# Other PSUM banks for the last 20 steps, products moved behind P V, x loaded in chunks, splits parted anew, and Q/K rows stored so that a head is one transfer

## The chip, the cores and the metric

The kernel runs on one core of a Trainium2 chip. A core has a matrix engine (TensorE, "PE" in the profile), a vector engine (VectorE, "DVE"), an engine for activations (ScalarE, "ACT"), a general one (GpSimd, "POOL") and one that mostly issues transfers (SyncE, "SP"). They run side by side and wait for each other by semaphores. Matrix products are written to PSUM, which has eight banks; 128 rows of 512 float32 numbers fill one. The metric is device time in microseconds (us), the median of several runs; lower is better.

## The reference, cut to what matters

One input `x` of 2048 tokens and 512 features goes through two branches, mixed by a gate for each token:

```
g = sigmoid((x * gate_w).sum(-1, keepdims=True))
# branch a: attention, 32 heads of 16 features, softmax over all 2048 keys
q, k, v = split(x @ wqkv)
p = softmax(q @ k.T / 4)            # for each head, 2048 x 2048
a = (p @ v) @ wo
# branch b: the two tokens of highest score r = x @ w_r get an FFN, the others pass
y = (silu(x_sel @ w_gate) * (x_sel @ w_up)) @ w_down * sigmoid(r_sel)
b = x, with y added at the two tokens
out = g * a + (1 - g) * b
```

Nearly all of the work is the scores, their exponentials and P V: 32 heads with 2048 x 2048 scores each.

## The kernel before, in words

**Number format.** Products that need more than the matrix engine's fast float32 form are made of parts: an operand is split into a high part and the rest (`split`: ScalarE makes the high part, VectorE or GpSimd subtracts), and high x high, low x high and high x low are added up in PSUM. So a projection or an output product is 3 matmuls per 128 rows of the inner dimension.

**Start.** `load_x` fetches x transposed in four blocks of 512 tokens, each in four pieces of 128 x 512 from a matrix with rows of 2048 tokens; SP issues all of them, between the two halves of the first weights. `split_x` splits each piece, three on VectorE and the fourth on GpSimd. Fourteen matmuls on zeros (L228) run while the first data arrive. `proj` makes K and Q of the first 8 heads for a block of tokens (12 matmuls, an eviction with a split of the result, `ev`). The V weights are split once the first three projections are recorded (L254). Then 21 lead steps hold the row maxima of the first unit (`m_lead`) and the V products (`v_part`).

**Main part.** Heads go in pairs and queries in halves: 32 units, each of 16 steps over 128 keys, 512 steps in all. A step `s` makes S^T for 128 keys and 1024 queries of the two heads: four matmuls (`s_piece`, L669), with two heads in the two row halves of the array, and one exponential (ScalarE, L670) for each, into `P[s]`. P V (`av_mm`) follows two steps later. The row maxima that the softmax subtracts are found ahead, from products of their own (`m_piece`, L589) that VectorE reduces (L593). `ORDER` writes out the order of S^T pieces (s), maxima (m), P V (A) and fillers (f). A filler is a part of other work: the projections of later heads, the small FFN, the output products with `wo`.

**PSUM.** The tiles are: `st`, three banks; `mxa`, one tile of two banks; `mxb`, `fl` and `av`, one bank each. In the main part S^T uses `st`, the maxima use `mxa` and `mxb`, fillers use `fl` and P V uses `av`.

**The last 20 steps.** When the maxima are done (steps 492 to 511), a loop of its own makes the four S^T pieces of a step, P V of two steps earlier, and in every second step a filler between the second and the third piece; there they are output products of the last heads (`wo_last`), which VectorE adds to the result (`finish`). The fourth piece of each step goes into `mxb`, the others into `st`: four banks.

**End.** `tail` makes the last normalisation and the products of the last heads' output. Blocks 10 and 11 go through the two halves of `mxa`, block 9 through `st`; then four blocks, each of three products (high part, low part, high part), a finish and a store.

**Transfers.** Q and K go through a scratch in DRAM, a plane of high parts and a plane of low parts. A matmul needs each head's rows three times 16: for K high, low, high, for Q high, high, low. `load_k` and `load_q` make that of two transfers for each head, one of 32 rows and one of 16. Each queue issues its transfers in program order, and the order of work between engines comes from a layer that records which instruction reads and writes which tile and sets the waits.

## Time and profile before

| | us |
|---|---|
| median of three runs | 1420.77 (1420.66 to 1420.93) |
| the profiled execution | 1419.9 |
| its span, which the trace covers | 1417.9 |
| first to last matmul of the start, before the maxima (0 to 27.2) | 27.2 |
| lead steps (27.2 to 91) | 63.8 |
| main part (91 to 1359) | 1268.0 |
| last 20 steps' S^T (1359 to 1402.1) | 43.1 |
| end (1402.1 to 1417.9) | 15.8 |

In the span TensorE has 1410.2 us of busy time (99%), VectorE 1288.8 (91%), ScalarE 1170.9 (83%) and GpSimd 320.4 (23%). How to read the rows: in rows in order of time the first number is the start in us, the second the length, then the engine, the line, the operation, output and inputs by the program's names, and the count where rows were merged. What stands in brackets is the idle time of the engine before it and what ended it. Starts and ends of matmuls overlap, as they are pipelined.

### The profile page before, as it was taken

What the parts mean: (1) busy time and instruction counts of PE and PEld (TensorE: products, weight loads), DVE (VectorE), ACT (ScalarE), POOL (GpSimd) and SP (SyncE); (2) the same over time, 40 slices, a digit from 0 to 9 for tenths busy, and PEclk for the clock granted to TensorE, in tenths of its full rate; (3) what the DMA queues carried; (4) which work ended last, traced back from release to release, by engine and by line L of the source; (5) the groups of instructions that cost most, each with busy time, mean ns of one, the idle gap of its engine ahead of it and who ended that gap; (6) DMA issues with size and microseconds to landing.
All of it is one profiled execution on the core that took longest, in us unless ns stands there. A gap on an engine that the chain in (4) does not pass through costs nothing.

```text
span 1417.9 us, 24172 instructions
## 1 busy us (share of the span) xinstructions
PE 1410.2 (99%) x9113; PEld 630.7 (44%) x9113; DVE 1288.8 (91%) x1532; ACT 1170.9 (83%) x2276; POOL 320.4 (23%) x337
## 2 busy tenths in 40 slices
PE   9999999999999999999999999999999999999998
PEld 6654444444444444444444444434444444444433
DVE  6889999999999999999999999999999999999943
ACT  5568888888888888888888888888888888888986
POOL 4851101102000001200000100043722322234411
PEclk9999999999999999999999999999999999999999
DMA  8601121212223221312222332424322131012012
GB/s 242 235 27 51 30 42 31 66 34 51 46 64 97 62 54 31 68 30 65 58 83 54 87 82 78 105 58 120 83 46 54 34 69 28 26 31 58 10 35 93
DMA packets 51592, 92.87 MB, mean 65 GB/s; under 512 B 14208, under 2 KB 21376, under 8 KB 49844
## 3 DMA queue, kind: packets, MB, share of 16 engines
q1 hardware_dynamic: 51188, 91.02, 24.4%
q8 instruction: 72, 1.18, 0.4%
q0 software_dynamic: 288, 0.30, 0.1%
q14 instruction: 44, 0.36, 0.1%
HBM read 63.77 MB, written 28.57 MB: 65 GB/s over the span
## 4 chain that ended last, share of the span: by engine, by line
PE 98%; DVE 0%; DMA 0%; ACT 0%; SPq 0%; issue 0%; POOL 0%; DVEq 0%; ACTq 0%
PE av L679 36%; PE st L669 24%; PE mxa L589 12%; PE mxb L589 10%; PE fl L154 6%; PE fl L508 4%; PE st L298 3%; PE st L154 2%; PE mxa L624 1%; PE fl L399 1%; DMA xs<-xT 0%; PE fl L437 0%; DVE acc L559 0%; DVE Mr L593 0%; PE mxa L508 0%; PE mxb L624 0%
## 5 line engine op out<-in xcount | busy, mean ns | idle before, releaser
L670 ACT ACTIVATE P<-st 128x512 f32<-128x512 f32 x2028 | 1065.6, 599 | 191.4 <-PE st L669 108.0
L593 DVE TENSOR_REDUCE Mr<-mxa 128x2 f32<-128x1024 f32 x655 | 795.7, 1215 | 2.6 <-PE mxa L589 2.5
L679 PE MATMUL av<-P,V 128*32 128x512 f32 x4096 | 545.6, 605 | 0.0
L669 PE MATMUL st<-Qx,Kx 50*128 50x512 f32 x2028 | 536.5, 444 | 0.8 <-ACT P L670 0.6
L593 DVE TENSOR_REDUCE Mr<-mxb 128x1 f32<-128x512 f32 x654 | 450.9, 689 | 61.0 <-PE st L669 17.1
L669 PEld LDWEIGHTS st<-Qx,Kx 50*128 50x128 f32 x2028 | 279.0, 184 | 239.6 <-ACT P L670 223.8
L589 PE MATMUL mxb<-Kx,Qx 48*128 48x512 f32 x654 | 325.1, 497 | 0.0
L589 PE MATMUL mxa<-Kx,Qx 48*128 48x512 f32 x1310 | 294.7, 417 | 0.0
L589 PEld LDWEIGHTS mxb<-Kx,Qx 48*128 48x128 f32 x654 | 119.5, 183 | 273.7 <-DVE Mr L593 273.7
L589 PEld LDWEIGHTS mxa<-Kx,Qx 48*128 48x128 f32 x1310 | 124.8, 183 | 43.6 <-DVE Mr L593 2.6
L679 PEld LDWEIGHTS av<-P,V 128*32 128x32 f32 x4096 | 81.2, 108 | 139.3 <-issue 133.2
L205 POOL TENSOR_SCALAR ev<-pe 128x512 fp32r<-128x512 f32 x24 | 35.7, 1490 | 411.6 <-ACT pe L203 411.6
L475 POOL TENSOR_TENSOR acc<-acc,w 128x512 f32<-128x512 f32 x36 | 46.1, 1280 | 202.1 <-ACT w L474 202.0
L77 POOL TENSOR_SCALAR hl<-m 128x16 fp32r<-128x16 f32 x31 | 7.8, 252 | 294.1 <-DVE m L640 294.1
L154 PE MATMUL fl<-xh,wh 128*128 128x512 f32 x96 | 42.9, 447 | 0.0
L154 PE MATMUL fl<-xh,wl 128*128 128x512 f32 x96 | 40.4, 421 | 0.0
L508 PE MATMUL fl<-woh,ahl 128*128 128x512 f32 x96 | 35.2, 447 | 0.0
L559 DVE SCALAR_TENSOR_TENSOR acc<-fl,gg,acc 128x512 f32<-128x512 f32 x11 | 8.2, 747 | 27.9 <-PE fl L508 27.9
L629 DVE TENSOR_REDUCE Mr<-mxa 128x2 f32<-128x1024 f32 x21 | 25.7, 1222 | 8.4 <-PE mxa L624 8.4
L154 PE MATMUL fl<-xl,wh 128*128 128x512 f32 x96 | 32.6, 421 | 0.0
L300 ACT ACTIVATE V<-st 128x512 f32<-128x512 f32 x16 | 9.6, 600 | 27.8 <-PE st L298 27.8
L206 POOL TENSOR_TENSOR ev<-pe,ev 128x512 fp32r<-128x512 f32 x24 | 30.8, 1284 | 2.0
(192 smaller groups left out, 780.0 us busy)
## 6 DMA issues: line engine op xcount, KB each, us to landing
q_scr<-ev SPq DMA_DIRECT2D x15, 512.0 KB
Kx<-k_scr SPq DMA_DIRECT2D x30, 256.0 KB
Qx<-q_scr SPq DMA_DIRECT2D x54, 128.0 KB
k_scr<-ev SPq DMA_DIRECT2D x13, 512.0 KB
Qx<-q_scr SPq DMA_DIRECT2D x70, 64.0 KB
xs<-xT SPq DMA_DIRECT2D x16, 256.0 KB
xn<-x SPq DMA_DIRECT2D x4, 1024.0 KB
Qx<-hr SPq DMA_DIRECT2D x256, 2.0 KB
```

The source lines that it names most:

```text
L154: nc.tensor.matmul(ps, a[:, i, c, :], b[nb][:, c, :], start=n == 0, stop=n == 11)
L205: nc.gpsimd.tensor_scalar(ev[:, 0], t, 1.0, None, op0=OP.mult)
L206: nc.gpsimd.tensor_sub(ev[:, 1], t, ev[:, 0].bitcast(F32))
L298: nc.tensor.matmul(ps, a[nb][:, c, sl], b[:, c, :], start=c == 0 and n == 0, stop=c == 3 and n == 2)
L475: nc.gpsimd.tensor_add(a, a, w)
L508: nc.tensor.matmul(ps, a[:, sl], b[:a.shape[0], c, :], start=first and n == 0, stop=last and n == 2)
L589: nc.tensor.matmul(dst, Qx[u % 3][64 * j:64 * j + 48, t * 128:t * 128 + 128], k_of(u, t // 4)[64 * j:64 * j + 48, c * 512:c * 512 + 512], ...
L593: nc.vector.tensor_reduce(Mr[:, g0:g0 + (2 if r == 1 else 1)], MX[r - 1], axis=AX.X, op=OP.max, negate=True)
L629: nc.vector.tensor_reduce(*r, axis=AX.X, op=OP.max, negate=True)
L669: nc.tensor.matmul(ps, k, q, start=True, stop=True)
L670: nc.scalar.activation(P[s][:, 2 * j + c, :], ps, AF.Exp)
L679: nc.tensor.matmul(AV[0][32 * ct:32 * ct + 32, :], V[:, kt, h * VW:h * VW + 32], P[s][:, ct, :], start=kt == 0, stop=kt == KT - 1)
```

## The change

- **Banks of the last 20 steps.** S^T now goes through six banks in turn, two for each half of a step: two of `st`, then one of `st` and `mxb`, then the two halves of a `mxa` tile.
- **Products.** In these steps the filler comes after P V instead of between the second and the third S^T piece.
- **x.** The host lays x out in contiguous chunks of 128 x 512. Two of the first four chunks are issued by ScalarE.
- **Splits.** All four pieces of x are split by ScalarE and VectorE. The V weights are split in two halves, after the projections of K block 2 and K block 3, with the low part on GpSimd.
- **Scratch.** It holds three rows for each feature in the order in which they are needed, so that each head's 48 rows are one transfer (but for the first pair's Q, whose scratch is read as before in two). A store is two transfers instead of one, and writes a third row.
- **Smaller ones.** Ten matmuls on zeros instead of fourteen; `split_at` of the first output group three steps later; in `tail` block 11 finished by VectorE alone, the high products of two blocks ahead of the low ones, and the last block finished and stored in two halves over two queues.

```diff
-    qk_scr = {n: dram.tile([2, D, S], F32R, name=f"{n}_scr") for n in "qk"}
+    qk_scr = {n: dram.tile([D, 3, S], F32R, name=f"{n}_scr") for n in "qk"}
...
         for c in range(4):
-            nc.sync.dma_start(xst[nb][:, c], ap(xT, c * 128 * S + nb * 512, [[S, 128], [1, 512]]))
+            eng = nc.scalar if nb == 0 and c % 2 == 0 else nc.sync
+            eng.dma_start(xst[nb][:, c], ap(xT, (nb * 4 + c) * 128 * 512, [[512, 128], [1, 512]]))
...
-            split(xh[nb][:, c], xl[nb][:, c], xst[nb][:, c], lo_engine=nc.gpsimd if c == 3 else None)
+            split(xh[nb][:, c], xl[nb][:, c], xst[nb][:, c])
...
     def store_ev(g, which, nb, ev):
-        nc.sync.dma_start(
-            ap(qk_scr[which], g * 128 * S + nb * 512, [[S, 128], [D * S, 2], [1, 512]]).bitcast(F32), ev.bitcast(F32))
+        e = ev.bitcast(F32)
+        for i, src in ((0, e), (2, e[:, 0, :])) if which == "k" else ((0, e[:, 0:1, :].to_broadcast([128, 2, 512])), (2, e[:, 1, :])):
+            d = ap(qk_scr[which], (g * 384 + i) * S + nb * 512, [[3 * S, 128], [S, 2 - i // 2], [1, 512]])
+            nc.sync.dma_start(d.bitcast(F32), src)
...
-    for _ in range(14):
+    for _ in range(10):
         nc.tensor.matmul(wps, warm[:, :128], warm, start=True, stop=True)
...
-    for c in range(4):
-        split(wv[1][:, c], wv[2][:, c], wvs[:, c], lo_engine=nc.gpsimd if c % 2 else None)
...
-            nc.sync.dma_start(t[64 * j:64 * j + 32, :], ap(qk_scr["k"], o, [[S, 16], [D * S, 2], [1, S]]).bitcast(F32))
-            nc.sync.dma_start(t[64 * j + 32:64 * j + 48, :], ap(qk_scr["k"], o, [[S, 16], [1, S]]).bitcast(F32))
+            nc.sync.dma_start(t[64 * j:64 * j + 48, :], ap(qk_scr["k"], o, [[S, 48], [1, S]]).bitcast(F32))
...
     def s_piece(s, j, c):
...
-        ps = mxb_tile() if s > STEPS - LEAD and c == 1 and j == 0 else st_tile()
+        n = (2 * s + c) % 3
+        if s <= STEPS - LEAD or n == 0 or (n == 1 and j):
+            ps = st_tile()
+        elif n == 1:
+            ps = mxb_tile()
+        else:
+            if j:
+                MX[2] = mxa_tile()
+            ps = MX[2][:, 1 - j]
         nc.tensor.matmul(ps, k, q, start=True, stop=True)
         nc.scalar.activation(P[s][:, 2 * j + c, :], ps, AF.Exp)
...
         late_wo(1)
-        acc_add(11, pw[1], gg)
+        finish(11, pw[1])
...
-        for t in range(4):
-            for n, (a, b) in enumerate(((0, 0), (1, 0), (0, 1))):
-                nc.tensor.matmul(banks[t], hl[a][:, t * 128:t * 128 + 128], wz[0][:, b, :], start=n == 0, stop=n == 2)
-            finish(12 + t, banks[t])
-            store(12 + t)
+        for t, n in ((0, 0), (0, 1), (1, 0), (1, 1), (0, 2), (1, 2), (2, 0), (2, 1), (2, 2), (3, 0), (3, 1), (3, 2)):
+            a, b = ((0, 0), (0, 1), (1, 0))[n]
+            nc.tensor.matmul(banks[t], hl[a][:, t * 128:t * 128 + 128], wz[0][:, b, :], start=n == 0, stop=n == 2)
+            if n == 2 and t < 3:
+                finish(12 + t, banks[t])
+                store(12 + t)
+        a = acc[3][:, 3, :]
+        for i, eng in enumerate((nc.scalar, nc.sync)):
+            c = slice(256 * i, 256 * i + 256)
+            nc.vector.scalar_tensor_tensor(a[:, c], banks[3][:, c], gg[:, 15:16], a[:, c], op0=OP.mult, op1=OP.add)
+            eng.dma_start(out[15 * 128:, c], a[:, c])
...
-        at_step(now[0] + 10, split_at, 0, (0, 1))
+        at_step(now[0] + 13, split_at, 0, (0, 1))
...
     for w, nb in (("k", 2), ("k", 3), ("q", 1), ("q", 2)):
         proj0(w, nb)
+        if w == "k":
+            for c in (2 * nb - 4, 2 * nb - 3):
+                split(wv[1][:, c], wv[2][:, c], wvs[:, c], lo_engine=nc.gpsimd)
...
             start_step(s)
             for i in range(4):
-                if i == 2 and (s - count["s"] // 4) % 2 == 0:
-                    next(fills, None)
                 s_piece(s, 1 - i % 2, i // 2)
         p_v(s - 2)
+        if (s - count["s"] // 4) % 2 == 0 and s < STEPS:
+            next(fills, None)
         end_step(s)
...
-        "xT": np.ascontiguousarray(x.T), "x": x, "wqkv": wqkv,
+        "xT": np.ascontiguousarray(x.T.reshape(4, 128, 4, 512).transpose(2, 0, 1, 3)), "x": x, "wqkv": wqkv,
```

More of the change, by code (lines that the diff above doesn't have):

```diff
@@ L260, in load_k @@
         for j in range(2):
-            o = (g * 128 + r + 16 * j) * S
+            o = (g * 128 + r + 16 * j) * 3 * S
             t = Kx[pair % 2 if pair < PAIRS - 1 else 2].bitcast(F32)
-            nc.sync.dma_start(t[64 * j:64 * j + 32, :], ap(qk_scr["k"], o, [[S, 16], [D * S, 2], [1, S]]).bitcast(F32))
-            nc.sync.dma_start(t[64 * j + 32:64 * j + 48, :], ap(qk_scr["k"], o, [[S, 16], [1, S]]).bitcast(F32))
+            nc.sync.dma_start(t[64 * j:64 * j + 48, :], ap(qk_scr["k"], o, [[S, 48], [1, S]]).bitcast(F32))
     def load_q(u):
@@ L271, in load_q @@
             for j in range(2):
-                o = (pair * 32 + 16 * j) * S + q0
+                o = (pair * 32 + 16 * j) * 3 * S + q0
                 t = Qx[u % 3][:, i * n:i * n + n].bitcast(F32)
-                nc.sync.dma_start(t[64 * j:64 * j + 32], ap(qk_scr["q"], o, [[S, 16], [0, 2], [1, n]]).bitcast(F32))
-                nc.sync.dma_start(t[64 * j + 32:64 * j + 48], ap(qk_scr["q"], D * S + o, [[S, 16], [1, n]]).bitcast(F32))
+                if pair:
+                    nc.sync.dma_start(t[64 * j:64 * j + 48], ap(qk_scr["q"], o, [[S, 48], [1, n]]).bitcast(F32))
+                else:
+                    nc.sync.dma_start(t[64 * j:64 * j + 32], ap(qk_scr["q"], o, [[3 * S, 16], [S, 2], [1, n]]).bitcast(F32))
+                    nc.sync.dma_start(t[64 * j + 32:64 * j + 48], ap(qk_scr["q"], o + 2 * S, [[3 * S, 16], [1, n]]).bitcast(F32))
     def k_of(u, c):
@@ L667, in s_piece @@
         q = Qx[u % 3][64 * j:64 * j + 50, c * 512:c * 512 + 512]
-        ps = mxb_tile() if s > STEPS - LEAD and c == 1 and j == 0 else st_tile()
+        n = (2 * s + c) % 3
[3 more added lines that the diff above has]
+            ps = mxb_tile()
+        else:
+            if j:
+                MX[2] = mxa_tile()
+            ps = MX[2][:, 1 - j]
         nc.tensor.matmul(ps, k, q, start=True, stop=True)
```

## The prediction

> **What bounds the kernel now.** I read the page first, then the busy time by stage, then the instructions in order of time at both ends, where the edits lie.

> ```profile
> span 1417.9 us, 24172 instructions
> PE 1410.2 (99%) x9113; PEld 630.7 (44%) x9113; DVE 1288.8 (91%) x1532; ACT 1170.9 (83%) x2276; POOL 320.4 (23%) x337
> ```

> ```profile
> 8.75:27.20 18.45, 18.45 (x78) 14.32 (x78) 13.22 (x18) 12.71 (x23) 12.19 (x12) 1.00 0.92 296
> 91.00:1359.00 1268.00, 1267.35 (x8413) 550.12 (x8412) 1204.28 (x1415) 1077.92 (x2076) 256.73 (x280) 1.00 0.22 56
> 1359.00:1402.10 43.10, 43.03 (x266) 15.71 (x262) 9.86 (x15) 38.96 (x77) 1.29 (x1) 1.00 0.17 60
> ```

> The rows of the second fence are stages: start and end, length, busy time of PE, PEld, DVE, ACT and POOL, granted clock, DMA share, GB/s. TensorE is busy in all of them, so what counts is any moment in which an edit makes it wait or spares it work. The middle stage (1268.00 us) loses 0.65 us to waits in total: nothing there can be won. The last 20 steps, S^T 492 to 511, are the stage of 43.10 us: TensorE 43.03, ScalarE 38.96. ScalarE is close behind, and that matters below.

> Two steps of that stage and the start of a third, in order of time (start, length), first TensorE, then ScalarE with its group from the page:

> ```profile
> 1366.08 0.50 PE L669 MATMUL st<-Qx,Kx 50*128 50x512 f32 x2
> 1366.42 0.40 PE L669 MATMUL mxb<-Qx,Kx 50*128 50x512 f32 x1
> 1366.42 0.39 PE L669 MATMUL st<-Qx,Kx 50*128 50x512 f32 x1
> 1366.75 1.06 PE L679 MATMUL av<-P,V 128*32 128x512 f32 x8
> 1367.75 0.50 PE L669 MATMUL st<-Qx,Kx 50*128 50x512 f32 x2
> 1368.18 0.74 PE L508 MATMUL fl<-woh,Kx 128*128 128x512 f32 x2
> 1368.76 0.39 PE L508 MATMUL fl<-wol,Kx 128*128 128x512 f32 x1
> 1369.08 0.50 PE L669 MATMUL st<-Qx,Kx 50*128 50x512 f32 x1
> 1369.08 0.50 PE L669 MATMUL mxb<-Qx,Kx 50*128 50x512 f32 x1
> 1369.51 1.07 PE L679 MATMUL av<-P,V 128*32 128x512 f32 x8
> 1370.51 0.72 PE L669 MATMUL st<-Qx,Kx 50*128 50x512 f32 x3
> ```

> ```profile
> 1366.62 1.58 ACT L670 ACTIVATE P<-st 128x512 f32<-128x512 f32 x3 [0.34 <-PE st L669]
> 1368.06 0.62 ACT L670 ACTIVATE P<-mxb 128x512 f32<-128x512 f32 x1
> 1368.54 1.67 ACT L670 ACTIVATE P<-st 128x512 f32<-128x512 f32 x3
> ...
> L670 ACT ACTIVATE P<-st 128x512 f32<-128x512 f32 x2028 | 1065.6, 599 | 191.4 <-PE st L669 108.0
> ```

> A step without an output product runs from 1366.08 to 1367.75: 1.67 us, two pairs of S^T matmuls (0.34 and 0.33; the two of a pair run side by side in the two row halves of the array) and P V (1.00). A step with one runs from 1367.75 to 1370.51: 2.76, so the product costs 1.09. ScalarE begins an exponential 0.54 after its matmul began (1366.08 to 1366.62), needs 0.48 for each in a row (1368.06 to 1368.54), and one lasts 0.60 (599 ns). It waits for TensorE once per two steps (0.34), so TensorE is the bound.

> **The tail: what is added.** Two of the six banks are the halves of one tile, `mxa`. A pair of S^T products goes into both halves, and between the two the code records the exponential that reads the first half. The program as built carries a wait before the second product of each such pair, for exactly that exponential: the order of work is kept by tile, not by half. Before has one place with the same shape, the two late products in `tail()`, and its rows show what such a wait does:

> ```profile
> 1405.09 0.72 PE L508 MATMUL mxa<-woh,lahl 128*128 128x512 f32 x2
> 1405.65 0.39 PE L508 MATMUL mxa<-wol,lahl 128*128 128x512 f32 x1
> 1405.88 1.04 PE L795 MATMUL st<-cst,o 128*128 128x4 f32 x8
> ...
> 1406.08 0.75 DVE L559 SCALAR_TENSOR_TENSOR acc<-mxa,gg,acc 128x512 f32<-128x512 f32 x1 [5.20 <-PE mxa L508]
> ...
> 1406.88 0.74 PE L508 MATMUL mxa<-woh,lahl 128*128 128x512 f32 x2
> ```

> VectorE reads the first half until 1406.08 + 0.75 = 1406.83; the product into the second half begins at 1406.88, 0.05 later. TensorE had other work until about then, so this row alone doesn't prove the wait; it fits it, and gives 0.05 as the price from reader's end to product's start.

> So a pair in `mxa` is no longer side by side. In the best case (ScalarE idle) its second product begins 0.54 + 0.60 + 0.05 = 1.19 us after the first. TensorE takes its matmuls in order, so the next S^T pair, P V and the output product all stand behind it, and ScalarE idles too, since what it would read next is the product that waits for it.

> The banks run through three kinds of step. X (st st, st mxb) needs no such wait: 1.67. Y (mxa mxa, st st): second product at 1.19, 0.23 for itself (the spacing of matmuls in a row, 1405.65 to 1405.88), 0.34 for the pair, 0.99 for P V: 2.75, or 1.08 more. When no output product stood before Y, ScalarE still has the four exponentials of X: begun at -1.13, -0.65, -0.17 and 0.31 against Y's start, it is free at 0.79 instead of 0.54, so Y is 1.33 longer. Z (st mxb, mxa mxa): exponentials at 0.54 and 1.02 go ahead, that of `mxa` begins at 1.50 and ends at 2.10, the second product starts at 2.15; with 0.23 and 0.99 that is 3.37, or 1.70 more. Steps 492 to 511 are X Y Z in turn, and products follow the even ones, so six steps hold 1.08 + 1.33 + 2 x 1.70 = 5.81; three such rounds are 17.43, and steps 510 and 511 (X, then Y behind a product) add 1.08. Sum for 13 pairs: +18.5 us.

> **The tail: what is removed and moved.** Ten output products go from between two S^T pairs to behind P V. Before, each costs 1.09. Behind a P V the nearest row is the first late product: 1405.09 to 1405.88, 0.79; I add 0.06 for the change back to S^T (the product at 1368.76 takes 0.32, 0.09 over 0.23, so between 0 and 0.09). 0.85 against 1.09, ten times: -2.4. Its `fl` bank is freed by one VectorE finish of 0.75 per two steps, far off. Six banks would also let ScalarE lag by six exponentials instead of four; with TensorE as the bound that is worth nothing by itself, but without it the moved product would make S^T wait. Tail in all: +16.1.

> **The start.** x in chunks, two of the first four issued by ScalarE, VectorE instead of GpSimd for each fourth split, four warm matmuls fewer, the splits of the V weights later and on GpSimd.

> ```profile
> 0.73 1.28 ACT L70 ACT_TABLE_LOAD   x1 [0.73 <-PEq L1045]
> ...
> 1.18 1.85 SPq L138 DMA_DIRECT2D xs<-xT  x4
> ...
> 3.46 0.63 ACT L70 ACTIVATE wh<-ws 128x512 fp32r<-128x512 f32 x1 [1.45 <-DMA ws<-wqkv]
> ...
> 8.07 0.63 ACT L70 ACTIVATE xh<-xs 128x512 fp32r<-128x512 f32 x1 [0.70 <-DMA xs<-xT]
> 8.75 0.50 PE L154 MATMUL st<-xh,wh 128*128 128x512 f32 x1 [0.59 <-ACT xh L70]
> 8.78 1.29 POOL L71 TENSOR_TENSOR xl<-xs,xh 128x512 fp32r<-128x512 f32 x1 [3.14 <-ACT xh L70]
> ...
> 9.32 1.30 PE L154 MATMUL st<-xl,wh 128*128 128x512 f32 x4
> ...
> 10.46 0.40 PE L154 MATMUL st<-xh,wh 128*128 128x512 f32 x1
> ...
> 13.90 2.00 DVE L71 TENSOR_TENSOR xl<-xs,xh 128x512 fp32r<-128x512 f32 x3
> ...
> 31.54 0.50 PE L298 MATMUL st<-Kx,xh 128*128 128x512 f32 x1
> ```

> The fourth chunk lands at about 8.05 and sets 8.75, from which TensorE runs through. SP issues the four in 1.85; two on ScalarE's queue take half of that, 0.93, off the issue. There they delay its table load (0.73 + 0.93 + 1.28 = 2.94), which is still over before its first work at 3.46. The chunks land slower than they are issued (the last is issued by 3.03), so between 0 and 0.93 is won; I take 0.4, near the middle. Fewer warm matmuls are priced at nothing, since the wait for this chunk covers them.
> [...]
> The fourth split on VectorE (0.67, from 2.00 for three) instead of 1.29 lets the four xl matmuls run in 4 x 0.23 = 0.92 instead of the 1.14 from 9.32 to 10.46: -0.2. Against it VectorE then has four splits and an eviction, 4 x 0.67 + 0.6 = 3.3 us, per projection of 2.7 (12 x 0.23), over three projections: up to 1.7 of lag, which three `st` banks, each needed again only two projections later, should cover. The V weights' splits on GpSimd are 4 x 1.29 = 5.2, begun once K block 2 is out; first needed after 31.54, so hidden, and what queues behind them on GpSimd, the issue of Q's rows of block 1, is wanted later still. Start: -0.6, between -1.1 and +1.7.

> **The middle.** A head's rows in one transfer: K and Q loads fall from four issues to two, each store is two issues instead of one, 256 KB more written per store. Nothing waits on them in a stage with 0.65 us of loss and 0.22 DMA share. The later `split_at` passes one small GpSimd pair. Zero, at worst 1.

> **The end.** The finish of block 11 moves to VectorE, where its 0.75 fits into the 0.99 of idle time before the scaling (the first row below); the last block's finish and store are halved over two queues.

> ```profile
> 1408.60 0.42 DVE L810 TENSOR_TENSOR o<-o,mxb 128x256 f32<-128x256 f32 x1 [0.99 <-PE mxb L807]
> ...
> 1410.34 0.50 PE L820 MATMUL st<-wz,onl 128*128 128x512 f32 x1 [0.27 <-DVE onl L71]
> ...
> 1411.11 0.75 DVE L559 SCALAR_TENSOR_TENSOR acc<-st,gg,acc 128x512 f32<-128x512 f32 x1 [0.49 <-PE st L820]
> ...
> 1413.17 0.75 DVE L559 SCALAR_TENSOR_TENSOR acc<-mxb,gg,acc 128x512 f32<-128x512 f32 x1
> ```

> The first finish still needs a low-part product, now fifth instead of third but without the 0.27 wait: about 1411.1 as before, and VectorE's four finishes in a row end at about 1413.9 as before. From there to 1417.9 is 4.0 us of store; the last piece is half as large. Between 0 and 1.0, I take 0.4.

> **Sum.** The profiled execution took 1419.9 us, 0.9 (0.06%) under the median of 1420.77, too little to correct for. 1419.9 + 16.1 - 0.6 - 0.4 = 1435.0; I forecast 1435, some 1% slower.

> **Rivals.**
> It is faster: the wait is satisfied before it is reached, pairs in `mxa` start together like those at 1366.08, and six banks work as meant. 1419.9 - 2.4 - 0.6 - 0.4 = 1416.5. The place is the second `mxa` product; gains of 3.4 over 13 pairs mean that the change breaks even at 0.26 us per pair. Against it: its exponential cannot begin before 0.54. Chance 0.05.
> Every pair costs only the idle case, because stalls let ScalarE catch up more than I count: 13 x 1.08 = 14.0 instead of 18.5, so 1430.5. Chance 0.20.
> Every pair costs as much as Z, because the queue of exponentials never empties: 13 x 1.70 = 22.1, so 1438.6. For it: ScalarE's 38.96 of 43.10. Against: each stall idles it too. Chance 0.15.
> TensorE's clock drops in the broken tail. The granted clock is 1.00 in all three stages quoted, with hardly a gap. Of the 43.03 us of matmuls a third at half clock would add 14: 1449. Chance 0.04.
> [...]
> My forecast: 0.55; the last 0.01 is no change.

> **Range.** 1430 to 1440 takes in the two rivals beside the forecast, with the start's and the end's bounds; below lies the faster case, above the clock. Within 0.2% (2.8 us), about what a measurement here can tell from no change: 0.01; faster 0.05; slower 0.94.

> **What would show it.** In the tail, 13 single `mxa` products each 1.2 to 1.8 us after the other, TensorE's waits there released by ScalarE's `P`, 16 us more between the first and the last S^T of steps 492 to 511, and ScalarE's busy share down to about 65%. At the start the first unbroken matmul at about 8.35; the middle stage unchanged to 1 us. Wrong would be pairs of `mxa` starting together, or a middle stage that stretches.

## The result, and the profile after

| | before | after |
|---|---|---|
| median of five runs, us | 1420.77 (1420.46 to 1421.91) | 1443.37 (1440.57 to 1446.10) |
| profiled execution | 1419.9 | 1443.37 |
| its span | 1417.9 | 1441.6 |

The changed kernel takes 1.0163 times as long (95% interval 1.0150 to 1.0175). The direction and the waits of the pairs were forecast, the fall of the clock was not; the time lies 8.4 us above the forecast and 3.4 above the range.

First the stages of both traces: start and end, length, busy time of PE, PEld, DVE, ACT and POOL, granted clock, DMA share, GB/s. The cuts are the first product of the maxima, the first S^T of step 492 and the first product after the last P V. Before:

```profile
0.00:27.26 27.26, 25.49 (x98) 17.14 (x98) 16.22 (x23) 17.15 (x29) 17.18 (x20) 1.00 0.85 268
27.26:1358.96 1331.70, 1330.90 (x8693) 591.50 (x8692) 1256.72 (x1484) 1109.81 (x2161) 299.37 (x314) 1.00 0.24 61
1358.96:1405.09 46.13, 46.06 (x291) 16.54 (x287) 9.90 (x15) 40.91 (x80) 1.29 (x1) 1.00 0.17 59
1405.09:1417.90 12.81, 7.78 (x40) 5.49 (x37) 5.97 (x11) 3.01 (x6) 2.59 (x2) 0.90 0.38 143
```

After:

```profile
0.00:25.30 25.30, 24.12 (x94) 17.15 (x95) 15.23 (x25) 16.97 (x29) 11.52 (x16) 1.00 0.86 301
25.30:1356.81 1331.51, 1330.70 (x8693) 589.99 (x8692) 1256.80 (x1484) 1110.21 (x2161) 301.32 (x317) 1.00 0.25 67
1356.81:1429.08 72.27, 57.56 (x290) 18.66 (x287) 9.90 (x15) 42.49 (x81) 1.28 (x1) 0.88 0.11 37
1429.08:1441.60 12.52, 7.51 (x41) 5.50 (x37) 6.43 (x13) 2.35 (x5) 1.29 (x1) 0.94 0.40 148
```

The third row is the whole loss: the last 20 steps went from 46.13 to 72.27 us, 26.1 more. TensorE now has 14.7 us of idle time there, but its busy time grew too, from 46.06 to 57.56, for the same matmuls, and the granted clock is 0.88 instead of 1.00. (Part of that growth is not the clock: a product that no longer runs beside its partner adds busy time too. In the filled kernel below, at full clock, it is 58.04, of which 30 added matmuls of 0.23 make 6.9.) The start gained 1.96, the end 0.29, the middle 0.19. These make the 23.7 us by which the spans differ.

A step of kind Z in the changed kernel (its second pair of S^T products goes into `mxa`), TensorE in order of time, and then what TensorE waited for in the last 20 steps (sum, count, longest):

```profile
1361.88 0.49 PE L680 MATMUL st<-Qx,Kx 50*128 50x512 f32 x1
1361.89 0.50 PE L680 MATMUL mxb<-Qx,Kx 50*128 50x512 f32 x1
1362.22 0.39 PE L680 MATMUL mxa<-Qx,Kx 50*128 50x512 f32 x1
1364.10 0.50 PE L680 MATMUL mxa<-Qx,Kx 50*128 50x512 f32 x1 [1.49 <-ACT P L681]
1364.53 1.54 PE L690 MATMUL av<-P,V 128*32 128x512 f32 x8
1366.01 1.22 PE L511 MATMUL fl<-woh,Kx 128*128 128x512 f32 x2
```

```profile
PE mxa L680 <- ACT P L681: 14.5, 13, 1.5
```

The second product of the pair starts 1.88 after the first, released by ScalarE, 13 times in all. What the forecast did not count is in the last two rows, in which the clock falls: a P V that takes 1.06 before takes 1.54 here, and the two high products 1.22 instead of 0.74. The same trace in stretches of 3.41 us, chosen to begin and end with the fall of the clock behind that pair:

```profile
1361.57:1364.99 3.42, 1.93 (x13) 0.64 (x12) 0.00 (x0) 2.69 (x6) 0.00 (x0) 1.00 0.01 1
1364.99:1368.40 3.41, 3.41 (x15) 1.33 (x7) 0.71 (x1) 0.25 (x1) 0.00 (x0) 0.50 0.02 5
...
1382.05:1385.47 3.42, 1.93 (x12) 0.56 (x12) 0.00 (x0) 2.95 (x6) 0.00 (x0) 1.00 0.35 110
1385.47:1388.88 3.41, 3.41 (x12) 1.03 (x11) 0.00 (x0) 0.60 (x1) 0.00 (x0) 0.50 0.00 0
...
1395.71:1399.12 3.41, 2.10 (x15) 0.65 (x15) 0.67 (x1) 1.94 (x5) 0.00 (x0) 1.00 0.23 82
1399.12:1402.53 3.41, 2.72 (x17) 1.11 (x15) 1.08 (x2) 2.58 (x5) 0.26 (x1) 1.00 0.00 0
1402.53:1405.95 3.42, 2.03 (x14) 0.45 (x11) 0.00 (x0) 3.10 (x6) 1.02 (x1) 1.00 0.20 77
1405.95:1409.36 3.41, 3.31 (x11) 1.11 (x12) 0.00 (x0) 0.65 (x2) 0.00 (x0) 0.50 0.00 0
1409.36:1412.77 3.41, 3.41 (x15) 0.90 (x13) 0.75 (x1) 1.66 (x4) 0.00 (x0) 0.50 0.20 77
...
1416.19:1419.60 3.41, 1.92 (x11) 0.82 (x13) 0.75 (x1) 1.78 (x5) 0.00 (x0) 1.00 0.20 77
1419.60:1423.01 3.41, 3.41 (x16) 0.70 (x12) 0.00 (x0) 1.48 (x3) 0.00 (x0) 0.50 0.00 0
```

All the falls fit one grid: each begins a whole number of 3.413 us behind 1364.99 (6, 12 and 16 of them) and lasts one or two. In them the clock is exactly 0.50. Five such stretches, 17.1 us, do work for which full clock would need about half the time (a P V that lies whole in one, 1385.70 to 1387.56, takes 1.86 from its start to the next, against 1.00 at full clock). That makes 8.5 us an estimate from above: while TensorE is slow, ScalarE catches up, and some waits get shorter. (The second product of the pair behind the longest fall comes 1.18 after the first, 1413.03 to 1414.21; in the filled kernel below the same pair takes 1.54.)

The times of the five runs say the same. Their mean granted clocks over the whole kernel are 0.996 at 1440.57 us, 0.995 at 1442.04, 0.994 at 1443.37 and 0.991 at 1445.98 and 1446.10. A straight line through them reaches full clock at about 1436.7, so the clock costs the median run some 6.7 us; this is an estimate, as the clocks are known to 0.001, or 1 us.

### The profile page after: what moved, and what is told of

It reads as the page before. It is cut to its first block, busy times and chain, and to the rows that moved or that the text cites. A ratio compares the mean times of both kernels' runs of the same rounds, so it can differ in the third digit from the quotient of the medians.

```text
span 1441.6 us, 24092 instructions
## 1 busy us (share of the span) xinstructions
PE 1419.9 (98%) x9109; PEld 631.3 (44%) x9109; DVE 1288.4 (89%) x1536; ACT 1172.0 (81%) x2275; POOL 315.4 (22%) x334
## 3 DMA queue, kind: packets, MB, share of 16 engines
q8 instruction: 72, 1.18, 0.4%
## 4 chain that ended last, share of the span: by engine, by line
PE 98%; ACT 1%; DVE 0%; issue 0%; DVEq 0%; ACTq 0%
PE av L690 36%; PE st L680 23%; PE mxa L592 12%; PE mxb L592 10%; PE fl L155 6%; PE fl L511 4%; PE st L301 3%; PE st L155 2%; ACT P L681 1%; PE mxa L627 1%; PE mxa L680 1%; PE fl L402 0%; PE st L232 0%; PE fl L440 0%; DVE acc L562 0%; PE mxa L511 0%
## 5 line engine op out<-in xcount | busy, mean ns | idle before, releaser
L303 ACT ACTIVATE V<-st 128x512 f32<-128x512 f32 x16 | 9.6, 600 | 27.3 <-PE st L301 27.3
```

## The experiments

**The cause of the loss: four kernels.** The theory (A): the wait in the `mxa` pairs makes the idle times, and these bring the clock down. The rival (B): something else in the new tail is slow, the moved products or the banks themselves.

*One wait taken away.* The order of recording is changed: both products of an `mxa` pair, then both exponentials. Six banks and everything else stay.

```diff
         nc.tensor.matmul(ps, k, q, start=True, stop=True)
-        nc.scalar.activation(P[s][:, 2 * j + c, :], ps, AF.Exp)
-        o_half()
+        both = s > STEPS - LEAD and n == 2
+        if both and j:
+            return
+        for i in (1, 0) if both else (j,):
+            nc.scalar.activation(P[s][:, 2 * i + c, :], MX[2][:, 1 - i] if both else ps, AF.Exp)
+            o_half()
```

> The changed kernel with one edit: both matmuls of an mxa pair are recorded ahead of both exponentials, so that the second product has no wait for the first exponential. Six banks, products behind P V, start, scratch and end stay. Theory A (the wait in the mxa pairs makes the stalls, and the stalls make the clock drop): last 20 steps back to some 44 us (72.3 after the change, 46.1 before, first S^T to last P V), granted clock 1.00 there, and the start's 2.2 us and the end's 0.3 stay: 1416 to 1418 us. Theory B (something else in the new tail is slow, such as the product behind P V or the use of mxa and mxb for S^T): tail over 55 us, total over 1428.

Measured: 1415.42 us, 0.9962 of before (0.9948 to 0.9976), 28 us less than the changed kernel and 5.4 less than the kernel before that ran beside it (1420.83). The last 20 steps as a stage, and two steps of them on TensorE:

```profile
1356.88:1401.16 44.28, 44.07 (x291) 14.66 (x287) 9.90 (x15) 40.36 (x80) 1.28 (x1) 1.00 0.17 61
```

```profile
1365.11 0.50 PE L680 MATMUL mxa<-Qx,Kx 50*128 50x512 f32 x2
1365.44 0.40 PE L680 MATMUL st<-Qx,Kx 50*128 50x512 f32 x2
1365.77 1.07 PE L694 MATMUL av<-P,V 128*32 128x512 f32 x8
1366.77 0.74 PE L511 MATMUL fl<-woh,Kx 128*128 128x512 f32 x2
1367.35 0.40 PE L511 MATMUL fl<-wol,Kx 128*128 128x512 f32 x1
1367.67 0.50 PE L680 MATMUL st<-Qx,Kx 50*128 50x512 f32 x1
```

The two `mxa` products are one row again (x2), the step without a product takes 1.66 (1365.11 to 1366.77) and the product behind P V costs 0.90 (1366.77 to 1367.67). Theory B falls: the rest of the change is a gain.

*Four banks, products moved.* The changed kernel with the banks of before.

```diff
-        n = (2 * s + c) % 3
-        if s <= STEPS - LEAD or n == 0 or (n == 1 and j):
...
-            ps = MX[2][:, 1 - j]
+        ps = mxb_tile() if s > STEPS - LEAD and c == 1 and j == 0 else st_tile()
```

> The changed kernel with the four banks of before (three of st and mxb for the fourth piece); the products stay behind P V, and start, scratch and end stay. Theory A: no mxa pair, so no stall of 1.5 us and no lower clock. Four banks let ScalarE lag by four exponentials only, so a product behind P V lets it run dry: some waits of TensorE for banks, together no more than 4 us more than before in the last 20 steps: 1416 to 1422 us. Theory B (the moved products are what is slow): over 1428.

Measured: 1421.81, 1.0006 of before (0.9996 to 1.0016); the last 20 steps 50.51, 4.4 more than before (at most 4 was expected) and 6.2 more than with six unbroken banks. Three rows of TensorE, and below them one of ScalarE:

```profile
1356.98:1407.49 50.51, 50.51 (x290) 17.06 (x286) 9.91 (x15) 40.37 (x80) 1.28 (x1) 1.00 0.15 53
```

```profile
1365.78 1.00 PE L672 MATMUL st<-Qx,Kx 50*128 50x512 f32 x3
1366.77 0.50 PE L672 MATMUL mxb<-Qx,Kx 50*128 50x512 f32 x1
1367.20 1.07 PE L682 MATMUL av<-P,V 128*32 128x512 f32 x8
```

```profile
1366.10 0.62 ACT L673 ACTIVATE P<-mxb 128x512 f32<-128x512 f32 x1
```

Four S^T products take 1.42 here (1365.78 to 1367.20) instead of 0.66 above. The one into `mxb` begins at 1366.77, 0.05 after ScalarE is done with the one before it in that bank (1366.10 + 0.62). The row of the stage calls TensorE busy throughout: these short waits show only as a longer distance between starts.

*Six banks alone.* The kernel before with the choice of banks of the change, products in the middle of the step.

```diff
-        ps = mxb_tile() if s > STEPS - LEAD and c == 1 and j == 0 else st_tile()
+        n = (2 * s + c) % 3
+        if s <= STEPS - LEAD or n == 0 or (n == 1 and j):
...
+            ps = MX[2][:, 1 - j]
```

> The kernel before with the choice of six banks alone; products between the second and the third S^T piece as before, start, scratch and end as before. Theory A: the wait is there as in the changed kernel, so the last 20 steps cost some 18 us more by the pairs' stalls, and 6 to 10 more if the clock falls: 1438 to 1448 us. Theory B (the six banks are harmless, the moved products or another part cost the time): within 4 us of 1420.8.

Measured: 1453.49 (1442.28 to 1458.04), 1.0238 of before (1.0220 to 1.0255): more than the 1438 to 1448 expected, and widely spread. The profile is that of the run of 1442.28. There TensorE waits for ScalarE 13 times as well, but 1.49 or 1.50 only three times, and behind two of these the clock falls for 3.41 us each. The six runs' mean granted clock is 0.997 at 1442.28 and 0.983 at 1456.87 and 1458.04. So the banks alone cause the loss; why the clock falls more often in some runs of this kernel than in the changed one, no profile of such a run shows.

*The idle time filled.* The changed kernel with five more products ahead of the second product of each Z pair.

```diff
+        if s > STEPS - LEAD and n == 2 and c and not j:
+            z = fl_tile()
+            for i in range(5):
+                nc.tensor.matmul(z, lastp[0][0][:, :128], wop[0][:, 3, :], start=True, stop=True)
         nc.tensor.matmul(ps, k, q, start=True, stop=True)
```

> The changed kernel with five more matmuls (128 x 512, 0.23 us each, into fl, used for nothing) ahead of the second mxa product in every third step (seven steps), where TensorE stands idle for 1.49 us. The output is unchanged, only work is added. Theory A (idle times of 1.5 us bring the clock down): with the idle times filled the granted clock stays near 1.00 in the last 20 steps, and these get 7 to 9 us shorter although work is added: about 1435 us. Rival (the clock falls for another reason, or the idle times of the other steps suffice): the clock still falls to 0.5 to 0.6 in places and the time stays at 1441 to 1446.

(There are six such steps, not seven.) Measured: 1436.33 (1436.17 to 1436.65), 1.0110 of before (1.0093 to 1.0126). With 30 matmuls more it is 7.0 us faster than the changed kernel, the four runs are 0.5 us apart instead of 5.5, and the clock stays up:

```profile
1356.72:1421.90 65.18, 58.04 (x321) 21.88 (x317) 9.90 (x15) 42.38 (x80) 1.28 (x1) 1.00 0.12 42
```

This parts the loss. Without the waits 44.28, with them at full clock 65.18, with the falls 72.27: the pairs cost 20.9 and the clock 7.1, which agrees with the 6.7 from the line through the five runs. The added matmuls hardly disturb this: the second product of a Z pair starts 1.88 to 1.94 after the first here, 1.88 in the changed kernel.

**How much idle time brings the clock down.** Three kernels. In the first only the seven Y pairs keep the exponential between their products (idle times up to 1.04 in the changed kernel), in the second only the six Z pairs (`and not c` in place of `and c`).

```diff
-        both = s > STEPS - LEAD and n == 2
+        both = s > STEPS - LEAD and n == 2 and c
```

> The changed kernel in which only the seven mxa pairs in the first half of a step (kind Y) have the exponential between their products; the six in the second half (kind Z) have both products ahead of both exponentials. In the changed kernel Y pairs left TensorE idle for 0.69 to 1.05 us and Z pairs for 1.49. Theory A (it takes an idle time above about 1.05 us to bring the clock down): granted clock 1.00 in the last 20 steps, and the pairs cost 1.2 to 1.5 us each, 9 in all, over the kernel without any wait (1415.4): about 1424 to 1426 us, with runs close together. Theory B (any broken pattern brings it down): dips below 0.7 and over 1428.

> The reverse: only the six pairs in the second half of a step (kind Z) wait, the seven in the first half don't. Theory A: idle times of about 1.49 us, 1.9 us for each pair, 11.5 in all, so 1427 us at full clock, and the clock falls to 0.5 to 0.6 behind some of them, which adds 3 to 12: 1430 to 1439, with runs apart by some us. Theory B (it takes both kinds of wait, or their number, to bring the clock down): clock 1.00, 1427 us, runs close together.

Measured: Y alone 1423.65 (1423.49 to 1424.00), 1.0024 of before (1.0014 to 1.0035), clock 1.00 in all nine runs, just under the time expected; the last 20 steps 52.98, so the seven pairs cost 8.7, with no idle time above 0.99. Z alone 1435.92 (1434.81 to 1436.57), 1.0111 of before (1.0094 to 1.0128), with three falls and idle times of 1.43 and 1.80. Here two stretches on its grid, each with the one behind it:

```profile
1361.98:1365.39 3.41, 1.98 (x11) 0.83 (x12) 0.00 (x0) 1.97 (x4) 0.00 (x0) 1.00 0.03 6
1365.39:1368.80 3.41, 3.41 (x26) 0.91 (x24) 0.75 (x1) 2.49 (x6) 0.00 (x0) 1.00 0.20 77
1368.80:1372.22 3.42, 1.99 (x11) 0.89 (x7) 0.75 (x1) 3.11 (x7) 0.00 (x0) 1.00 0.17 63
1372.22:1375.63 3.41, 3.41 (x13) 0.80 (x13) 0.69 (x1) 0.72 (x2) 0.00 (x0) 0.50 0.04 16
```

Both have 1.43 us of idle time; the clock falls behind the second only. Theory B falls in both: Y pairs never bring the clock down here, Z pairs do without them. But an idle time of that length does not always do it.

The third is the filled kernel with one added product instead of five.

```diff
-            for i in range(5):
+            for i in range(1):
```

> As the kernel with five added matmuls ahead of the second mxa product of the six Z pairs, but with one added matmul each, so that of 1.49 us of idle time about 1.2 is left (it is used for nothing and changes no output). Theory A with a bound near 1.49: clock 1.00 and about 1436 us as with five. Theory A with a bound near 1.05 to 1.2: the clock still falls and the time is 1440 to 1446.

Measured: 1438.16 (1437.01 to 1440.27), 1.0124 of before (1.0107 to 1.0141): between the two times expected. No idle time is longer than 1.06 now, and still the clock falls twice in the profiled run, the slowest of the four:

```profile
1380.49:1383.91 3.42, 2.36 (x17) 0.82 (x13) 0.00 (x0) 2.69 (x7) 0.00 (x0) 1.00 0.33 105
1383.91:1387.32 3.41, 3.41 (x13) 1.22 (x7) 0.28 (x1) 0.46 (x1) 0.00 (x0) 0.50 0.00 0
1400.97:1404.39 3.42, 2.35 (x14) 0.75 (x13) 0.00 (x0) 2.96 (x6) 0.65 (x1) 1.00 0.15 58
1404.39:1407.80 3.41, 3.41 (x24) 1.10 (x23) 0.75 (x1) 1.37 (x3) 0.00 (x0) 1.00 0.00 0
```

So there is no sharp bound on a single idle time. Cut on each trace's grid, the last 20 steps of the seven kernels profiled with six banks (after, the unbroken pairs behind P V, filled with five and with one, six banks alone, Y alone, Z alone) have 107 whole stretches at full clock. Of 81 with less than 0.99 us of idle time none is followed by a fall, of 15 with 0.99 to 1.2 two are, of 11 with more, nine. Behind the last P V stretches with 1.23 us (unbroken pairs) and 1.59 (Z alone) are followed by none, while the last falls that the traces show stand behind 2.09 us (the kernel before) or more. So idle time alone does not decide it, and what parts the cases in between stays open.

**The place of the products.** The kernel with unbroken pairs, products back in the middle of the step.

```diff
             for i in range(4):
+                if i == 2 and (s - count["s"] // 4) % 2 == 0:
+                    next(fills, None)
                 s_piece(s, 1 - i % 2, i // 2)
         p_v(s - 2)
-        if (s - count["s"] // 4) % 2 == 0 and s < STEPS:
-            next(fills, None)
```

> The kernel with the unbroken mxa pairs (both products ahead of both exponentials), and the output products back between the second and the third S^T piece as before the change. It prices the move of the products alone, against the same kernel with the products behind P V (1415.42 us, last 20 steps 44.28 us). Theory A (what the prediction says of the moved products): each costs 1.09 in the middle against about 0.90 behind P V, ten times, so the last 20 steps take about 46.1 and the whole about 1417.3 us. Rival (the place of the product is worth nothing, the 1.8 us came from the six banks): within 0.4 us of 1415.4.

Measured: 1416.66, 0.9975 of before (0.9965 to 0.9985); last 20 steps 46.05 against 44.28 with the products behind P V and 46.13 before. The stages say that the place is worth 1.8 and six unbroken banks nothing without it. The medians are 1.2 apart, but the two ran on different chips; each against the kernel before that ran beside it (1420.83 and 1420.03), they won 5.4 and 3.4, which is 2.0 apart. Four banks with moved products lost 4.4. The two belong together.

**The start.** Four kernels, each the kernel before with some of the edits there: all of them; chunks in one piece and two on ScalarE's queue; chunks in one piece alone; the second with ten matmuls on zeros. Layout, queue and zeros are these lines:

```diff
-            nc.sync.dma_start(xst[nb][:, c], ap(xT, c * 128 * S + nb * 512, [[S, 128], [1, 512]]))
+            eng = nc.scalar if nb == 0 and c % 2 == 0 else nc.sync
+            eng.dma_start(xst[nb][:, c], ap(xT, (nb * 4 + c) * 128 * 512, [[512, 128], [1, 512]]))
...
-    for _ in range(14):
+    for _ in range(10):
```

> The kernel before with the edits to the start alone: x in contiguous chunks, two of the first four issued by ScalarE, all four splits on VectorE, ten matmuls on zeros, the splits of the V weights later and on GpSimd. Tail, scratch and end as before. Theory A (the start gains what the traces of before and after show, 27.26 to 25.30): the first product of the maxima at 25.3 instead of 27.3 and 1418.5 to 1419.2 us in all. Rival (the forecast's 0.6): 1420.2 us.

> The kernel before with x in contiguous chunks and two of the first four chunks issued by ScalarE; splits, matmuls on zeros and V weights as before. If the earlier landing of the chunks carries the gain of the start: the first product of the maxima at about 25.5 to 25.8, 1419 us. If the fourth split on VectorE carries it: 26.6 or later, 1420.2 us or more.

> The kernel before with x in contiguous chunks alone, all issued by SP. If the layout makes the chunks land sooner (theory: long runs in memory): the fourth chunk's split on ScalarE begins by 7.5 instead of 8.07, and the first product of the maxima comes at 26.5 or earlier. If only the second queue does (rival: issue time): as before, 8.0 and 27.2, 1420.8 us.

> The kernel before with x in contiguous chunks, two of the first four issued by ScalarE, and ten matmuls on zeros instead of fourteen; splits of x and V weights as before. Theory A (once the chunks land early, the fourteen matmuls on zeros hold up the first product; with them it began at 6.63 us, right behind the last of them): first product at 5.6 to 5.8, first product of the maxima at 25.6 or so, 1418.2 to 1418.5 us. Rival (the split on VectorE and the V weights' splits make what load alone, 1418.8, lacks to all of the start's edits, 1418.2): 1418.8 and 26 or later.

| edits | us | against before | first product of the maxima |
|---|---|---|---|
| all of the start | 1418.17 | 0.9986 (0.9976 to 0.9995) | 25.45 |
| layout and second queue | 1418.78 | 0.9992 (0.9982 to 1.0001) | 27.14 |
| layout | 1419.59 (1418.18 to 1420.79) | 0.9996 (0.9986 to 1.0005) | 25.71 |
| layout, second queue, ten on zeros | 1418.90 | 0.9991 (0.9981 to 1.0001) | 25.90 |

Before is 1420.03 for the first three and 1420.41 for the last. All edits together win 1.9 us, as the traces said; the load alone 1.25, layout alone 0.4, both with intervals that reach past no change; smaller pieces can't be told apart. Times and last column disagree for layout and load, as the profiled executions are the fastest of one (1418.18) and the slowest of the other (1420.27). In that latter one the first product waits for no data, but for the matmuls on zeros. Here are its rows, and then the row of the same fourteen matmuls in the layout kernel:

```profile
1.18 5.80 PE L230 MATMUL st<-warm 128*128 128x512 bf16 x14 [1.18 <-DVE warm L227]
6.63 0.58 PE L155 MATMUL st<-xh,wh 128*128 128x512 f32 x1
...
24.20 0.50 PE L155 MATMUL st<-xh,wh 128*128 128x512 f32 x1 [0.87 <-DVE evx L74]
```

```profile
1.19 4.48 PE L229 MATMUL st<-warm 128*128 128x512 bf16 x14 [1.19 <-DVE warm L226]
```

The same fourteen took 5.80 and 4.48, and the product behind them begins at 6.63 and at 5.32. In the trace of before they start 0.43 us apart up to 5.42 and 0.22 apart from 5.70 on, the record of full clock begins at 5.55 between the two, and the product behind them comes at 6.17: until then TensorE runs at half its later pace. By the same two paces the change is put, as an estimate, at about 6.5 and 3.8 in the two traces above. (The traces hold no record of the clock before that moment, so the 1.00 of the first stage above says nothing of its first microseconds.) So single executions differ by over a microsecond at the start for a reason that is not in the edits, and the last column can't rank the smaller edits.

With ten of them the first product began at 5.78, as expected, but the time did not follow: 1.5 us under its before, not two, and no better than the rival's 1418.8. What is left to all edits, 0.4, may lie with VectorE, for which TensorE waits 0.87 in the last row and which in these kernels still splits two pieces of the V weights; the runs do not settle it. What the layout does is plainer in ScalarE's rows: the split of the fourth chunk ends at 8.70 before (8.07 + 0.63 in the forecast's row), at 7.29 with the layout alone and at 7.48 with the second queue as well.

## Why the prediction was wrong

**The tail's pairs: right in kind, 2.4 too small.** 13 pairs, each released by ScalarE: as forecast. From the first to the second product Y was forecast at 1.19, or 1.44 with ScalarE still busy, and Z at 1.81. Z took 1.88 above; two Y pairs of the filled kernel, the second behind an output product, took 1.54 and 1.19:

```profile
1367.98 0.49 PE L684 MATMUL mxa<-Qx,Kx 50*128 50x512 f32 x1
1369.52 0.49 PE L684 MATMUL mxa<-Qx,Kx 50*128 50x512 f32 x1 [1.05 <-ACT P L685]
...
1378.61 0.50 PE L684 MATMUL mxa<-Qx,Kx 50*128 50x512 f32 x1
1379.80 0.49 PE L684 MATMUL mxa<-Qx,Kx 50*128 50x512 f32 x1 [0.69 <-ACT P L685]
```

What else was mis-sized is the time behind the wait: the lone second product in front of P V was counted 0.23, and 1364.10 to 1364.53 is 0.43. The sum of +18.5 measured +20.9. By kind: Y alone 8.7 against 8.3 forecast, which leaves 12.2 against 10.2 for Z, if the two simply add up. The rival "idle case" (+14.0) fails by its sum. That of "all like Z" (+22.1) lies nearer to 20.9 than the forecast's; it fails by kind: seven Y pairs cost 8.7, not seven times 1.70, so Y and Z differ, as the forecast had it.

**The clock: the step that failed.** The forecast entered it at nothing, and gave a rival with a fall 4 in 100. That stalls of up to 1.6 us (Z's 1.81 less 0.23 for the product itself) leave the clock at 1.00 was the author's estimate; no run shows it. The clock measured +7.1. This alone moves the time out of the range: filled, with the waits kept and the clock at 1.00, the kernel takes 1436.33, 1.3 above the forecast. So the false step is that estimate: stalls of 1.49 us were enough here, and of 1.06 at most in the kernel filled with one product. The rival had the fall and twice the price: it put a third of the matmul time at half clock, which no run shows, +14 on top of the forecast's 1435; five stretches of 3.41 at half clock, 17.1 us of 72.27, cost about half of that. Its 1449 is 5.6 too high, the forecast 8.4 too low; its chance of 4 in 100 rested on the same estimate.

**Moved products: right.** 0.85 was forecast, 0.90 measured, so -1.8 instead of -2.4. That four banks would make S^T wait then is shown by 50.51.

**The start: too small.** -0.6 forecast, -1.96 in the trace and -1.9 in runs with the start's edits alone, outside the bounds. The forecast took the gain as issue time of two chunks (0.93 at most) and put the new layout at nothing. In the changed kernel all four chunks are there sooner:

```profile
4.92 2.42 ACT L70 ACTIVATE xh<-xs 128x512 fp32r<-128x512 f32 x4
```

```profile
1.18 4.45 PE L232 MATMUL st<-warm 128*128 128x512 bf16 x10 [1.18 <-DVE warm L229]
5.59 0.80 PE L155 MATMUL st<-xh,wh 128*128 128x512 f32 x1
```

ScalarE splits the four in one go, by 7.34, and TensorE runs unbroken from 5.59 (8.35 was forecast), right behind the last matmul on zeros. The layout alone brings the end of these splits from 8.70 to 7.29, and the second queue does not bring it further (7.48). What the second queue adds to the layout between the medians (1419.59 to 1418.78, 0.8) stays under the 0.93 of issue time, but is not clear of noise. By the medians the layout by itself, the matmuls on zeros and VectorE's share make up the other 1.1, of which the forecast had only 0.2, for VectorE; how these three share it is not shown.

**The middle and the end: right.** 0.2 less and 0.3 less against zero and -0.4. The last finish ends 8.8 us into its stage in both (1413.92 of 1405.09 before, 1437.90 of 1429.08 after), and the smaller store is over 3.70 later instead of 3.98:

```profile
1437.03 0.87 DVE L838 SCALAR_TENSOR_TENSOR acc<-mxb,gg,acc 128x256 f32<-128x256 f32 x2
```

The sum, in the order of the forecast: 20.9 - 1.8 + 7.1 - 2.0 - 0.2 - 0.3 = 23.7. Of what the forecast said would show it, the 13 releases by ScalarE came, and the pairs' distances (1.18 to 1.88 in the changed kernel); the last 20 steps grew by 26 us instead of 16, and ScalarE's busy share is 59% (42.49 of 72.27), not 65%.

## What to carry to other kernels

Where two halves of one tile take turns between engines, look at how the work is recorded: the order was kept by tile here, and recording both writers before both readers turned a loss of 1.6% into a gain of 0.4% with the same banks. A stall on TensorE is to be priced twice: its length, and the chance that it takes a stretch of half clock with it; in this kernel that was a third on top (7.1 on 20.9). And where buffers and order are changed together, price them together: more banks, with unbroken pairs, were worth nothing alone, later products lost 4.4 us alone, both gained 1.8.

## What the runs showed of the hardware

The place of a stall on the grid went with this. Of the six stalls of 1.49 us in the changed kernel's trace, the three that lie whole in one stretch are each followed by a fall; of the three that a boundary cuts in two (those that end at 1375.86, 1397.02 and 1406.05) only the last is. The runs spread too: five of the changed kernel, with mean clocks of 0.991 to 0.996, lie 5.5 us apart, nine of the kernel with the Y pairs alone, all at 1.00, 0.5. A spread that is new after an edit, with a mean clock below 1.00, is a sign to look for this.
